# One decode step: row sums of wq, gate, up, w_down and part of wo moved to VectorE, TensorE's projections put into one loop

## The chip, the cores and the metric

The kernel runs on one core of a Trainium2 chip. The core has TensorE (PE), VectorE (DVE), ScalarE (ACT), GpSimd (POOL), a sync engine (SP) that here only issues transfers, and 16 DMA engines that move data between HBM and the on-chip memory (SBUF, 128 partitions). The metric is device time of one execution in microseconds; lower is better. Before the change it is 1362.64 us, the median of 3 runs (1362.63 to 1363.09).

## The reference

One token of one sequence goes through attention over a cached K and V and, beside it, a gated feed-forward layer; all values are float32.

```python
x = A_x                                    # [1, 1, 576]
xn = _layernorm(x, axis=-1)
q = (xn @ wq).reshape(B, Sq, H, Dh)        # wq [576, 4096], H = 32, Dh = 128
scores = einsum("bhqd,bhkd->bhqk", q, k_cache) * (Dh ** -0.5)   # k_cache [1, 32, 16384, 128]
p = softmax(scores, axis=-1)
o = einsum("bhqk,bhkd->bhqd", p, v_cache)
a = o.reshape(B, Sq, H * Dh) @ wo          # wo [4096, 576]
h = gelu(xn @ w_gate) * (xn @ w_up)        # [576, 4608] each
b = h @ w_down                             # [4608, 576]
return x + a + b
```

The two caches are 268 MB each and are read once; all weights together are some 50 MB.

## The kernel before

**Slots.** Three buffers of 64 KB in each partition hold everything large: `sa`, `sb` (K, and weights before and after the heads) and `sv` (V, and weights before the first head). Weight matrices with 576 input rows are cut into 512 rows, four neighbouring ones to a partition (`wmain`, line 188), and the last 64 rows, the *tail*. The tail is folded so that each of its rows fills two partitions (`wtail`, line 189): 128 partitions by half a row.

**Loads.** All large loads go out on SP's queue in program order: wq main into `sa` (line 136), wq tail into `sb` (240), the fourth row and the tail of gate and of up into `sv` (243 to 247), the first three rows of gate into `sb` and of up into `sa` (`ffn`, 328), K of head 0 in two parts into `sb` (386), K of head 1 into `sa` (388), V of head 0 into `sv` (390). Then a loop over heads (391) waits for a free K slot (`s_kf`), loads K, waits for a free V slot (`s_vf`), loads V. After the heads come w_down (28 of its 36 rows into `sb`, line 472; the rest into `sa`, 481, whose last half row per partition is gathered by three small loads to 20 and 8 partitions, 486 to 488) and wo in pieces of 16, 8, 4, 2, 1, 1 rows (497). An engine that waits holds back everything behind it on its queue; SP's waits are those of `o.dma` (line 112) and `take` (360).

**Start.** x comes in on ACT's queue; layernorm runs on one partition; TensorE turns x into columns (288 to 292), and `project` (301) multiplies wq, gate and up by them with 32-column matmuls: 40 calls for wq, 60 each for gate and up, written out one after another. VectorE picks the valid part of each product out of PSUM (334) and reduces it (337).

**Heads.** For each of 32 heads VectorE multiplies K by q (425) and sums over the head dimension (427), takes the maximum (416, 418), ScalarE makes the exponentials (457), TensorE multiplies them by V (411) and folds the result into a column (`out_steps`, 352) in the next turn. TensorE's loop (400) starts at a block boundary of its program (`head_slot`).

**End.** VectorE sums 28 rows of w_down, each scaled by a column of `hT`, into `total` (473 to 476). TensorE multiplies the other rows of w_down (541 to 544) and all 32 rows of wo (545 to 555) by columns of `hT` and `oT`; most accumulate in two halves of 288 columns, the last 12 in four quarters of 144, into which VectorE first adds the halves (550, 551). VectorE and ScalarE copy the quarters out (557 to 562), ScalarE sends the result (563). `release` (149) is a two-turn loop at the end of the programs of VectorE and ScalarE with a branch hint to a place at their start.

**Bookkeeping.** `Order.op` (91) issues an instruction, finds by `needs` (63) what it must wait for and puts the waits on it; `dve`, `act`, `pe_op`, `load` (218 to 236) are short forms.

Of the kernel before, what the change touches and what calls it, by code (L numbers as in the profile page):

```python
# [9 lines left out]
AF = mybir.ActivationFunctionType  # L10
# [14 lines left out]
QG, QB = HD // 4, 512  # L25
QS = HD // 2
# [5 lines left out]
WO_PIECES = (16, 8, 4, 2, 1, 1)  # L32
WO_A = 16
WO_Q = 12
QUART = D // 4
FEW, EACH, RUN = 5, 4, 6
MANY, GROUP = FEW * EACH, EACH * RUN + 1
LEFT = P - FEW * EACH * RUN
AT = 32
SLOT_AT = 28672  # L40
# [3 lines left out]
class Order:  # L44
# [4 lines left out]
    def __init__(self, tc):  # L49
        self.tc, self.nc = tc, tc.nc  # L50
        self.sem = {e: tc.alloc_semaphore(f"s_{e}") for e in ("scalar", "vector", "tensor")}
# [76 lines left out]
def kernel(ctx: ExitStack, tc: tile.TileContext, x, k_cache, v_cache, wq, wo, wg, wu, wd, out):  # L128
# [7 lines left out]
    i = nc.sync.dma_start(slots[0], wq[:DM].rearrange("(p j) f -> p (j f)", j=DJ)).then_inc(ends, 64)  # L136
# [26 lines left out]
def decode(tc, x, k_cache, v_cache, wq, wo, wg, wu, wd, out, slots, s_ends):  # L163
    nc = tc.nc
    o = Order(tc)
    places = [e.mark_branch_hint_location() for e in (nc.vector, nc.scalar)]
# [22 lines left out]
    wtail = {n: w[DM:].rearrange("d (s f) -> (d s) f", s=2) for n, w in (("q", wq), ("g", wg), ("u", wu))}  # L189
# [5 lines left out]
    eps_t, par, same, quarter = sbuf("eps_t", P, 1), sbuf("par", P, 2), sbuf("same", P, 32), sbuf("quarter", P, 4)  # L195
# [11 lines left out]
    row1 = sbuf("row1", 1, D)  # L207
    sel_p, sel_r, sel_l = sbuf("sel_p", P, MANY), sbuf("sel_r", P, RUN), sbuf("sel_l", P, LEFT)
    few_w, few_h = sbuf("few_w", P, RUN), sbuf("few_h", P, RUN + 1)
# [28 lines left out]
    ROW3 = 3 * DF  # L238
    nc.tensor.wait_ge(s_ends, 64).then_inc(s_ends, -64)
    qt = load(sb[:, ROW3 : ROW3 + QS], wtail["q"])  # L240
    row3, tails, at = {}, {}, 0
    for n in "gu":
        s = sem()
        spent.append((s, 48))
        row3[n] = load(sv[:, at : at + DF], wmain[n][:, ROW3:], s, 32)
        tails[n] = load(sv[:, at + DF : at + DF + DF // 2], wtail[n], s, 32)
        at += DF + DF // 2

    xrow = sv[:1, ROW3 + FG : ROW3 + FG + D]
    o.op("vector", lambda e: e.memset(x2, 0.0), x2)  # L250
    s_x = sem()
    o.dma(xrow, xf, s_x, value=49, eng="scalar")
    for i in range(2):
        o.dma(x2[32 * i : 32 * i + 1, :], xf[:, i * HALF : (i + 1) * HALF], s_x, value=49, eng="scalar")
    o.op("vector", lambda e: e.memset(ident, 0.0), ident)
    o.wait("gpsimd", [ident], [ident])
    nc.gpsimd.affine_select(out=ident, in_=ident, compare_op=ALU.not_equal, fill=1.0, base=0,
                            pattern=[[-1, P]], channel_multiplier=1).then_inc(s_x, 1)
    o.note("gpsimd", s_x, 49, [], [ident])
    o.op("vector", lambda e: e.memset(ones, 1.0), ones)  # L260
    o.op("vector", lambda e: e.memset(eps_t, EPS), eps_t)
    s_ap, s_vp, s_pa, s_v, s_vf, s_kf, s_qf, s_qd = (tc.alloc_semaphore(f"h{n}") for n in range(8))
    s_k = [tc.alloc_semaphore(f"k{n}") for n in range(2)]
    for bank, s in ((PO, s_pa), (pc, None), (pq, None)):
        o.op("vector", lambda e, bank=bank: e.memset(bank, 0.0), bank, signal=s)
    dve("tensor_reduce", par, ident.rearrange("p (d s) -> p s d", s=2), axis=AX.X, op=ALU.add)
    dve("tensor_reduce", same, ident.rearrange("p (q r) -> p r q", q=4), axis=AX.X, op=ALU.add)
    dve("tensor_reduce", quarter, ident.rearrange("p (q r) -> p q r", q=4), axis=AX.X, op=ALU.add)

    grouped = ident[:, : FEW * GROUP].rearrange("p (q t) -> p q t", q=FEW)  # L270
    inner = grouped[:, :, : GROUP - 1].rearrange("p q (s r) -> p q s r", s=EACH)
    dve("tensor_reduce", sel_p.rearrange("p (q s) -> p q s", q=FEW), inner, axis=AX.X, op=ALU.add)
    dve("tensor_reduce", sel_r, inner.rearrange("p q s r -> p r q s"), axis=AX.XY, op=ALU.add)
    dve("tensor_copy", sel_l[:, :FEW], grouped[:, :, GROUP - 1])
    dve("tensor_copy", sel_l[:, FEW:], ident[:, FEW * GROUP :])

    stn = nc.vector.BN_STATS_DIM
# [21 lines left out]
    dve("tensor_copy", xtb.rearrange("p (s r) -> p s r", s=2), xt.unsqueeze(2).to_broadcast([P, 2, 32]))

    def project(dst, steps, group, sizes):
        for k, (j, rhs) in enumerate(steps):
            for b, size in enumerate(sizes):
                for q in range(4):
                    lo = q * group + sum(sizes[:b])
                    if j < DJ:
                        lhs = xnb[:, 32 * j : 32 * j + 32]
                    else:
                        lhs = xtb[:, 32 * (q // 2) : 32 * (q // 2) + 32]
                        lo -= q // 2 * 2 * group  # L310
                    pe_op(dst[32 * q : 32 * q + 32, 512 * b : 512 * b + size], lhs, rhs[:, lo : lo + size],
                          k == 0, k == len(steps) - 1)

    project(qb, [(DJ, qt)] + [(j, sa[:, j * HD : (j + 1) * HD]) for j in range(DJ)], QG, (QB, QB))
# [5 lines left out]
    act(qcur, q_part(0))  # L320
    pe_op(pq[:, :DH], ones[:1, :], qcur, True, True)
    act(qs, pq[:, :DH], signal=s_qd)
    act(qcur, q_part(1), signal=s_ap)

    def ffn(which):
        n, t = "gu"[which], (sb, sa)[which]
        steps = [(3, row3[n]), (DJ, tails[n])]
        load(t[:, :ROW3], wmain[n][:, :ROW3])
        project(pg, steps + [(j, t[:, j * DF : (j + 1) * DF]) for j in range(DJ - 1)], FG, FB)
        gm = sv[:, ROW3 : ROW3 + FG].rearrange("p (m t) -> p m t", t=WD_T)  # L330
        at = 0
        for b, size in enumerate(FB):
            m = size // WD_T
            dve("tensor_mul", gm[:, at : at + m, :], pg[:, 512 * b : 512 * b + size].rearrange("p (m t) -> p m t", t=WD_T),
                same[:, at : at + m].unsqueeze(2).to_broadcast([P, m, WD_T]))
            at += m
        dve("tensor_reduce", gu[:, which * WD_T : (which + 1) * WD_T], gm.rearrange("p m t -> p t m"), axis=AX.X, op=ALU.add)

    ffn(0)
    ffn(1)  # L340

    def ffn_act():
        g, u = gu[:, :WD_T], gu[:, WD_T:]
        t1, th, t2 = (tt[:, i * WD_T : (i + 1) * WD_T] for i in range(3))
        dve("tensor_mul", t1, g, g)
        dve("tensor_scalar", t1, t1, 0.044715, 1.0, op0=ALU.mult, op1=ALU.add)
        dve("tensor_mul", t1, t1, g)
        act(th, t1, AF.Tanh, scale=0.7978845608028654)
        dve("scalar_tensor_tensor", t2, th, 1.0, g, op0=ALU.add, op1=ALU.mult)
        dve("scalar_tensor_tensor", hT, t2, 0.5, u, op0=ALU.mult, op1=ALU.mult)  # L350

    def out_steps(h):
        return [(pc[:, :1], z[:, j * DH : (j + 1) * DH], same[:, j : j + 1], j == 0, j == 3) for j in range(4)]
# [6 lines left out]
    def take(e, s, n=1, base=0):  # L360
        e.wait_ge(s, base + n).then_inc(s, -n)  # L361

    def head(h):
        return bass.ds(h, 1)

    ffn_act()
    last_h = hT[:, WD_T - 1 :]
    many, left = slice(AT, AT + MANY), slice(AT, AT + LEFT)
    dve("tensor_scalar", few_w, sel_r, last_h, None, op0=ALU.mult)
    pe_op(pc[many, 8 : 8 + RUN], sel_p, few_w, True, True)  # L370
    pe_op(pc[left, 8 + RUN : 9 + RUN], sel_l, last_h, True, True)
# [103 lines left out]
    for j in range(1, WD_A):  # L475
        dve("scalar_tensor_tensor", total, first[j], hT[:, j : j + 1], total, op0=ALU.mult, op1=ALU.add)
# [119 lines left out]
```

## Time and profile before

| | before |
|---|---|
| time, median of 3 | 1362.64 us |
| span of the profiled execution | 1361.1 us |
| ScalarE busy | 68.7 us (5%) |
| GpSimd busy | 0.5 us, 5 instructions |
| TensorE weight loads | 162.1 us (12%) |
| mean granted TensorE clock | 0.630 of full speed |
| read from HBM | 587.60 MB |

The span runs from the first to the last instruction of one profiled execution; what lies around it is the 1.5 us by which the median is larger. A group in the profile is a line of the kernel, an engine, an operation, and what is written from what (out<-in) with partitions x elements; after a bar come busy time and the mean in nanoseconds. In a timeline a row begins with its start and its length in us. A DMA row gives the size of one transfer in KB of 1024 bytes and the time from issue to landing.

### The profile page before, as it was taken

The numbers are of one execution on the slowest core, as the hardware profiler recorded it, in microseconds if no ns is written. First come the engines' busy times: TensorE is split into PE (matmuls) and PEld (weight loads), VectorE is DVE, ScalarE is ACT, GpSimd is POOL, SyncE is SP. The second block draws the span as 40 slices with busy tenths as digits, with TensorE's granted clock in tenths as the row PEclk, the third lists the DMA queues.
The fourth block names the chain that finished last, engine by engine and source line by source line (L and its number), as shares of the span: only waits on it lengthen the run. The fifth ranks groups of instructions, "written<-read, shape, count | busy, mean of one in ns | idle before, by whom it ended". The sixth has DMA issues, their size and how long they took to land. (4 is left out here: it accounts for less than half of the span.)

```text
span 1361.1 us, 7832 instructions
## 1 busy us (share of the span) xinstructions
PE 449.2 (33%) x3032; PEld 162.1 (12%) x3032; DVE 1163.6 (85%) x210; ACT 68.7 (5%) x238; POOL 0.5 (0%) x5
## 2 busy tenths in 40 slices
PE   2531233323322333323223333233223333332237
PEld 1110111101111111101101111011111111011112
DVE  1069999999888888898888888998888889988884
ACT  0000000000000000000000000000000000000000
POOL 0000000000000000000000000000000000000000
PEclk9765666666556666665566666665566666655668
DMA  9999999999999999999999999999999999999998
GB/s 402 447 424 435 435 443 435 433 431 431 433 433 431 433 435 435 443 435 433 431 431 433 433 431 433 435 435 443 435 433 431 431 433 433 431 433 435 435 446 354
DMA packets 11962, 587.69 MB, mean 432 GB/s; under 512 B 1329, under 2 KB 1715, under 8 KB 1973
## 3 DMA queue, kind: packets, MB, share of 16 engines
q1 hardware_dynamic: 11949, 587.60, 99.7%
q8 instruction: 5, 0.08, 0.0%
q10 hardware_dynamic: 8, 0.01, 0.0%
HBM read 587.60 MB, written 0.00 MB: 432 GB/s over the span
## 5 line engine op out<-in xcount | busy, mean ns | idle before, releaser
L357 PE MATMUL po<-slot_v,pe 128*4 128x512 f32 x2048 | 294.4, 739 | 577.2 <-PEq L361 577.2
L425 DVE TENSOR_TENSOR slot_a<-slot_a,qs 128x16384 f32<-128x16384 f32 x16 | 275.6, 17225 | 34.8 <-DVEq L361 34.8
L425 DVE TENSOR_TENSOR slot_b<-slot_b,qs 128x16384 f32<-128x16384 f32 x15 | 258.4, 17225 | 31.9 <-DVEq L361 31.9
L427 DVE TENSOR_REDUCE scores<-slot_a 128x128 f32<-128x16384 f32 x16 | 275.5, 17220 | 2.3
L427 DVE TENSOR_REDUCE scores<-slot_b 128x128 f32<-128x16384 f32 x15 | 258.3, 17220 | 2.2
L357 PEld LDWEIGHTS po<-slot_v,pe 128*4 128x4 f32 x2048 | 56.7, 99 | 787.8 <-issue 787.8
L404 PE MATMUL pg<-ident,pm 128*1 128x128 f32 x32 | 11.9, 371 | 238.1 <-PEq L361 238.1
L450 ACT ACTIVATE z<-po 128x512 f32<-128x512 f32 x32 | 19.1, 597 | 829.1 <-ACTq L361 829.1
L357 PE MATMUL pc<-same,z 128*128 128x1 f32 x256 | 59.8, 355 | 0.0
L357 PEld LDWEIGHTS pc<-same,z 128*128 128x128 f32 x256 | 57.1, 328 | 0.5
L222 DVE TENSOR_TENSOR slot_v<-pg,same 128x396 f32<-128x396 f32 (+1 forms) x6 | 3.3, 558 | 52.2 <-PE pg L219 52.0
L404 PEld LDWEIGHTS pg<-ident,pm 128*1 128x1 f32 x32 | 2.5, 79 | 243.4 <-issue 243.4
L418 DVE TENSOR_REDUCE nm<-pg 1x1 f32<-1x128 f32 x32 | 8.9, 279 | 21.4 <-DVEq L361 21.4
L357 PE MATMUL pg<-nm,ones 1*128 1x1 f32 x64 | 17.7, 343 | 18.5 <-PEq L361 18.5
L222 DVE SCALAR_TENSOR_TENSOR slot_b<-slot_b,hT 128x576 f32<-128x576 f32 x27 | 22.1, 819 | 0.9
L357 PE MATMUL pqs<-qcur,ones 1*128 1x128 f32 x64 | 14.8, 312 | 21.9 <-PEq L361 20.7
L357 PEld LDWEIGHTS pg<-nm,ones 1*128 1x128 f32 x64 | 15.9, 306 | 27.8 <-issue 27.8
L455 ACT ACTIVATE nb<-pg 128x1 f32<-128x1 f32 x32 | 5.5, 171 | 241.1 <-ACTq L361 241.1
L222 DVE TENSOR_REDUCE scores<-slot_b 128x64 f32<-128x8192 f32 x2 | 17.4, 8686 | 0.1
L222 DVE TENSOR_TENSOR slot_b<-slot_b,qs 128x8192 f32<-128x8192 f32 x2 | 17.4, 8686 | 0.0
L416 DVE TENSOR_REDUCE pm<-scores 128x1 f32<-128x128 f32 x32 | 9.1, 286 | 8.2 <-DVEq L361 8.0
L357 PEld LDWEIGHTS pqs<-qcur,ones 1*128 1x128 f32 x64 | 9.6, 186 | 49.9 <-issue 49.9
(109 smaller groups left out, 158.9 us busy)
## 6 DMA issues: line engine op xcount, KB each, us to landing
slot_b<-in_A_k_cache_dram SPq DMA_DIRECT2D x2, 4096.0 KB, 23.8
slot_b<-in_B_w_down_dram SPq DMA_DIRECT2D x1, 8064.0 KB, 42.0
slot_b<-in_B_w_gate_dram SPq DMA_DIRECT2D x1, 6912.0 KB, 55.3
slot_a<-in_B_w_up_dram SPq DMA_DIRECT2D x1, 6912.0 KB, 37.4
slot_a<-in_A_wo_dram SPq DMA_DIRECT2D x1, 4608.0 KB, 36.5
slot_v<-in_B_w_gate_dram SPq DMA_DIRECT2D x1, 2304.0 KB, 28.8
slot_v<-in_B_w_up_dram SPq DMA_DIRECT2D x1, 2304.0 KB, 35.9
slot_b<-in_A_wo_dram SPq DMA_DIRECT2D x1, 2304.0 KB, 33.4
```

What stands on the lines that cost most here:

```text
L222: o.op("vector", lambda e: getattr(e, name)(out, *ins, **kw), out, *[a for a in ins if isinstance(a, bass.AP)], *[a for a in kw.values() i ...
L357: i = nc.tensor.matmul(dst, lhs, rhs, start=start, stop=stop)
L404: nc.tensor.transpose(pt[:1, :P], pm, ident).then_inc(s_pt, 1)
L416: nc.vector.reduce_max(pm, sc, axis=AX.X).then_inc(s_vp, 1)
L418: nc.vector.tensor_reduce(nm[:1], pt[:1, :P], axis=AX.X, op=ALU.max, negate=True).then_inc(s_vp, 1)
L425: nc.vector.tensor_mul(blk, blk, qs.unsqueeze(1).to_broadcast([P, R, DH])).then_inc(s_d, 1)
L427: nc.vector.tensor_reduce(sc, blk, axis=AX.X, op=ALU.add).then_inc(s_d, 1)
L450: nc.scalar.activation(z, PO, AF.Copy).then_inc(s_ap, 1)
L455: nc.scalar.activation(nb, pb[:, :1], AF.Copy, scale=SCALE).then_inc(s_a, 1)
```

## The change

- The 64 tail rows of wq, gate and up are no longer folded: each fills one partition, so these three loads (1024, 1152 and 1152 KB, as before) go to partitions 0 to 63. The wq tail is the first load; x goes on SP's queue behind it; gate's and up's fourth row and tail share one place in `sv`, so up's wait for gate's to be used.
- VectorE multiplies each weight row by its column of x and adds the rows up (`first`, `more`): five instructions for each of wq, gate and up over 4096 or 4608 elements. The sums lie in `C` (`sv`).
- TensorE adds `C` over the partitions with a matrix of ones, in one loop of three turns (wq, gate, up), 12 matmul calls a turn; a fourth semaphore counts hand-overs (`s_c`, `s_g`).
- GpSimd adds up what VectorE picked from PSUM (a tree of five additions for gate and for up), and computes gelu's arithmetic.
- In TensorE's head loop the folding of a head's result comes after its V product, in the same turn; the loop no longer starts at a block boundary.
- w_down's last 8 rows and wo's first 12 rows go to VectorE's `total` (`gather`); wo comes in pieces of 12, 8, 6, 4, 1, 1 rows; TensorE's quarters take the last 6. The three small loads are gone.
- The softmax sums are scaled once per partition by a matmul with `lx`; `oT` is scaled by VectorE.
- `release` is called for TensorE too. TensorE's program has 486 instructions.

```diff
-WO_PIECES = (16, 8, 4, 2, 1, 1)
-WO_A = 16
-WO_Q = 12
+WO_PIECES = (12, 8, 6, 4, 1, 1)
+WO_D, WO_A, WO_Q = 12, 20, 6
...
-    i = nc.sync.dma_start(slots[0], wq[:DM].rearrange("(p j) f -> p (j f)", j=DJ)).then_inc(ends, 64)
+    i = nc.sync.dma_start(slots[2][:TAIL, T_AT : T_AT + HD], wq[DM:]).then_inc(ends, 64)
...
-    wtail = {n: w[DM:].rearrange("d (s f) -> (d s) f", s=2) for n, w in (("q", wq), ("g", wg), ("u", wu))}
...
+    r3, tail, C = sv[:, :DF], sv[:TAIL, T_AT : T_AT + DF], sv[:, C_AT : C_AT + DF]
+    qt, q0 = sv[:TAIL, T_AT : T_AT + HD], sv[:, T_AT : T_AT + HD]
...
+    o.dma(xrow, xf, s_x)
+    load(sa, wmain["q"])
+    load(sb[:, : 3 * DF], wmain["g"][:, : 3 * DF])
...
+    def more(out, row, j, acc):
+        dve("scalar_tensor_tensor", out, row, xp[: row.shape[0], j : j + 1], acc, op0=ALU.mult, op1=ALU.add)
+    def first(row):
+        dve("tensor_scalar", row, row, xp[:, 0:1], None, op0=ALU.mult)
...
+    dve("tensor_scalar", qt, qt, x5, None, op0=ALU.mult)
+    more(rows[0], rows[0], 0, q0)
+    more(rows[0], rows[1], 1, rows[0])
+    more(rows[0], rows[2], 2, rows[0])
+    more(CQ[:, :, :QW], rows[3].rearrange("p (g c) -> p g c", g=4), 3, rows[0].rearrange("p (g c) -> p g c", g=4))
+    tell("vector", s_c, 2)
+    load_rest("g")
+    first(rows[0])
+    more(rows[0], rows[1], 1, rows[0])
+    more(rows[0], r3, 3, rows[0])
+    more(rows[0][:TAIL], tail, DJ, rows[0][:TAIL])
+    nc.vector.wait_ge(s_g, 1)
+    more(C, rows[2], 2, rows[0])
+    tell("vector", s_c)
+    load(sa[:, : 3 * DF], wmain["u"][:, : 3 * DF])
+    load_rest("u")
+    first(rows[0])
+    nc.vector.wait_ge(s_g, 2)
...
+            gps("tensor_add", dst, gm[:, :n], gm[:, n : 2 * n])
...
+    spread(0)
+    tell("vector", s_c)
+    more(C, rows[1], 1, rows[0])
+    more(C, rows[2], 2, C)
+    more(C, r3, 3, C)
+    more(C[:TAIL], tail, DJ, C[:TAIL])
+    tell("vector", s_c)
+    with nc.Fori(0, 3, engines=OrderedEngineSet([KIND["tensor"]])):
+        take(nc.tensor, s_c, 2)
+        for b, size in enumerate(FB):
+            for q in range(4):
+                lo = q * FG + sum(FB[:b])
+                i = nc.tensor.matmul(pg[32 * q : 32 * q + 32, 512 * b : 512 * b + size], ones[:, :32], C[:, lo : lo + size], start=True, stop=True)
+        i.then_inc(s_g, 1)
+        take(nc.tensor, s_t)
+        nc.tensor.matmul(pq[:, :DH], ones[:1, :], qfirst, start=True, stop=True).then_inc(s_b, 1)
...
+    nc.sync.wait_ge(s_g, 3)
     o.wait("sync", [], [sv])
     load_v(0)
...
+    nc.vector.wait_ge(s_g, 3)
+    spread(1)
...
+    with nc.Fori(0, H, engines=OrderedEngineSet([KIND["tensor"]])):
...
-        chain(out_steps(0), s_pa)
-        take(nc.tensor, s_ap)
         take(nc.tensor, s_v, 16)
         chain([(PO[32 * (k % 4) : 32 * (k % 4) + 4, :], pe[:, 4 * k : 4 * k + 4], sv[:, 512 * k : 512 * k + 512], k < 4, k >= 28)
                for k in range(32)], s_pa)
         nc.tensor.drain().then_inc(s_vf, 1)
+        take(nc.tensor, s_ap)
+        chain(out_steps(), s_pa)
...
-    o.dma(few[:, : RUN * HALF], by_q[:, : GROUP - 1, :], s_x, value=97)
-    o.dma(few[:FEW, RUN * HALF :], by_q[:, GROUP - 1, :], s_x, value=97)
-    o.dma(few[FEW:LEFT, RUN * HALF :], src[FEW * GROUP :], s_x, value=97)
...
+    rows = load_rows(sb, 0, wdv, 0, WD_A)
+    total = gather(rows, hT, None)
     take(nc.sync, s_vf)
     load_v(H - 1)
     take(nc.sync, s_kf)
+    gather(load_rows(sa, 0, wdv, WD_A, WD_T - WD_A), hT[:, WD_A:], total)
...
+    pe_op(pl, lx, ones[:, :1], True, True)
+    dve("reciprocal", rl, pl)
+    nc.vector.wait_ge(s_o, H)
+    dve("tensor_mul", onx.rearrange("p (h r) -> p h r", r=4), oall.unsqueeze(2).to_broadcast([P, H, 4]),
         quarter.unsqueeze(1).to_broadcast([P, H, 4]))
     pe_op(po, onx, same, True, True)
+    dve("tensor_scalar", oT, po, rl, None, op0=ALU.mult)
+    gather(wo_rows[:WO_D], oT, total)
+    halves = [(oT[:, j : j + 1], wo_rows[j]) for j in range(WO_D, WO_T - WO_Q)] + [(ones[:, :1], total)]
+    for n, (lhs, w) in enumerate(halves):
+        add_half(lhs, w, last=n >= len(halves) - 2)
...
+    release(nc, KIND["tensor"], nc.tensor, places[2])
```

More of the change, by code (lines that the diff above doesn't have):

```diff
@@ L260, in decode @@
[L260 to L266, printed above, removed]
@@ new lines, in decode, with load_rest @@
+    nc.vector.wait_ge(s_ends, 64).then_inc(s_ends, -64)
+    dve("tensor_scalar", qt, qt, x5, None, op0=ALU.mult)
+    rows = [sa[:, j * HD : (j + 1) * HD] for j in range(DJ)]
+    more(rows[0], rows[0], 0, q0)
[3 more added lines that the diff above has]
+    tell("vector", s_c, 2)
+    def load_rest(n):
+        s = sem()
+        spent.append((s, 48))
+        load(r3, wmain[n][:, 3 * DF :], s, 32)
+        load(tail, {"g": wg, "u": wu}[n][DM:], s, 32)
@@ L318, in q_part, with out_steps @@
         return qb[r : r + 1, lo : lo + DH]
[L320 to L352, printed above, removed]
+    nc.scalar.wait_ge(s_g, 1)
+    cuts = sorted({0, 512, QW, *(sum(FB[:b]) for b in range(1, 3))})
+    for lo, hi in zip(cuts, cuts[1:]):
+        b = max(b for b in range(3) if sum(FB[:b]) <= lo)
+        at = 512 * b + lo - sum(FB[:b])
+        act(qb[:, lo:hi], pg[:, at : at + hi - lo])
+    act(qfirst, q_part(0))
+    tell("scalar", s_t, 3)
+    nc.scalar.wait_ge(s_b, 1)
+    act(qs, pq[:, :DH])
+    tell("scalar", s_c)
+    tell("scalar", s_qd)
+    act(qcur, q_part(1))
+    tell("scalar", s_ap)
+    def out_steps():
         return [(pc[:, :1], z[:, j * DH : (j + 1) * DH], same[:, j : j + 1], j == 0, j == 3) for j in range(4)]
@@ L358, in chain @@
         i.then_inc(s, 1)
-    def take(e, s, n=1, base=0):
-        e.wait_ge(s, base + n).then_inc(s, -n)
     def head(h):
         return bass.ds(h, 1)
[L366 to L371, printed above, removed]
-    act(few_h[left, RUN:], pc[left, 8 + RUN : 9 + RUN])
-    act(few_h[many, :RUN], pc[many, 8 : 8 + RUN])
-    o.wait("tensor", [ident, ones, same], [pg, pc, PO, pq])
-    o.wait("vector", [qs], [S, pm, nm])
-    o.wait("scalar", [qb], [z, qs, nb, pe, lsum, oall, qcur])
     def load_k(h, dst, s):
@@ L396, in decode @@
             load_v(i * 2 + (1 + s))
-    (s_a, a_base), (s_pt, pt_base) = o.step("scalar"), o.step("tensor")
-    with nc.Fori(0, H, engines=OrderedEngineSet([KIND["tensor"]]), head_slot={KIND["tensor"]: 0}):
+    take(nc.vector, s_qd)
+    for src, sc in parts:
+        blk = src.rearrange("p (n d) -> p n d", d=DH)
+        dve("tensor_mul", blk, blk, qs.unsqueeze(1).to_broadcast([P, SUB, DH]))
+        dve("tensor_reduce", sc, blk, axis=AX.X, op=ALU.add)
+    tell("vector", s_kf)
+    tell("vector", s_qf)
+    nc.vector.wait_ge(s_g, 3)
+    spread(1)
+    g, u = gu[:, :WD_T], gu[:, WD_T:]
+    t1, th = (tt[:, i * WD_T : (i + 1) * WD_T] for i in range(2))
+    gps("tensor_mul", t1, g, g)
+    gps("tensor_scalar", t1, t1, 0.044715, 1.0, op0=ALU.mult, op1=ALU.add)
+    gps("tensor_mul", t1, t1, g)
+    o.wait("tensor", [ident, ones, same], [pg, pc, PO, pq])
+    o.wait("vector", [], [pm, nm])
+    o.wait("scalar", [], [z, nb, pe, ls, lx, oall])
+    s_pt, pt_base = o.step("tensor")
+    with nc.Fori(0, H, engines=OrderedEngineSet([KIND["tensor"]])):
         take(nc.tensor, s_ap)
```

211 lines of the change are left out of this document (86 added, 125 removed).

## The prediction

> **What bounds the kernel now.** The page comes first: its span, the busiest engines and the transfers.
>
> ```profile
> span 1361.1 us, 7832 instructions
> ...
> PE 449.2 (33%) x3032; PEld 162.1 (12%) x3032; DVE 1163.6 (85%) x210; ACT 68.7 (5%) x238; POOL 0.5 (0%) x5
> ...
> q1 hardware_dynamic: 11949, 587.60, 99.7%
> q8 instruction: 5, 0.08, 0.0%
> ```
>
> The queue that carries all large loads has kept the 16 DMA engines busy for 99.7% of the span. VectorE, the busiest engine, is busy for 85%. The stretches say whether that holds everywhere:
>
> ```profile
> 25.00:140.00 115.00, 46.49 (x384) 16.59 (x387) 60.20 (x25) 4.36 (x14) 0.00 (x0) 0.67 1.01 436
> 140.00:500.00 360.00, 117.45 (x731) 42.30 (x724) 334.58 (x40) 18.95 (x68) 0.00 (x0) 0.61 1.00 434
> 500.00:1250.00 750.00, 234.74 (x1467) 84.67 (x1467) 680.18 (x77) 38.26 (x137) 0.00 (x0) 0.61 1.00 435
> ```
>
> The columns are stretch, its length, PE, PEld, DVE, ACT and POOL with counts, granted clock, DMA share and GB/s. The rate is 434 to 436 GB/s in the projections (25 to 140 us), where DVE is busy for only 60.20 of 115 us, and through the heads. 435/16 is 27.2 GB/s for one engine. It is a ceiling: neither the work on chip nor the matrix being read moves it. The chain of work that ended last, and ScalarE's timeline at the end, close the picture:
>
> ```profile
> 1325.11 32.33 DMA slot_b<-in_A_wo_dram
> ```
> ```profile
> 1358.31 0.28 ACT L227 ACTIVATE row<-pqs 1x144 f32<-1x144 f32 x1 [13.56 <-PE pqs L219]
> 1358.69 0.28 ACT L227 ACTIVATE row<-pc 1x144 f32<-1x144 f32 x1
> 1359.01 0.24 ACTq L563 DMA_DIRECT2D out_dram<-row  x1
> ```
>
> The last piece of wo lands at 1357.44. Two final half rows, a copy and the 2.2 KB result follow, some 3.7 us. So the time is bytes over 435 GB/s plus a start of about 2 us and this end. The bytes do not change (all weights and caches are read once). What can change the time is therefore (1) the rate at which a transfer runs, (2) what else uses the DMA engines, (3) a compute step so late that SP's queue runs dry, (4) the end. Work taken off PE is worth nothing by itself.
>
> **The change part by part.** All sums are made against the profiled execution's 1361.1 us; the median of the runs lies 1.5 us higher, and I carry that difference over unchanged.
>
> *The tails (1).* The three tail loads, their KB and the us from issue to landing, in the transfer list of the first 100 us:
>
> ```profile
> slot_v<-in_B_w_gate_dram SPq DMA_DIRECT2D x1, 1152.0 KB, 31.1
> slot_v<-in_B_w_up_dram SPq DMA_DIRECT2D x1, 1152.0 KB, 39.5
> slot_b<-in_A_wq_dram SPq DMA_DIRECT2D x1, 1024.0 KB, 23.7
> ```
>
> Together 3328 KB, 3.41 MB, at 435 GB/s 7.8 us. Now they reach 64 partitions instead of 128. No row shows what that does: every large load of before reaches all 128. Bounds: if the ceiling belongs to the 16 engines and they stay evenly loaded, nothing (0 us). If it belongs to the receiving memory, or if engines are dealt out by partition, half of it is left, and each tail takes twice its time: +2.4, +2.7, +2.7, in all +7.8 us. A gain has no reason. The queue is full before and after each tail, so none of it can hide behind other transfers. The nearest rows are the stretches above: one ceiling for all shapes and loads, met only with all partitions in use. Of the three readings (memory side, engines by partition, engines alone) two give the upper end, and I take it: **+7.8 us**.
>
> [...]
>
> *Program and small loads (2).* The page's q8 row has 5 packets of 0.08 MB, 16 KB each: program, and of the engines only PE has a program of thousands of instructions. Spread evenly over 16 engines at 432 GB/s they cost 0.2 us; all on one engine of 27.2 GB/s, 3.0 us, for a load has landed only when its slowest engine is through. A program of 486 instructions should need none or one on the way. The three small w_down loads (144 KB to 20 and 8 partitions) vanish into a 128-partition load; being on few engines they cost up to about 1 us there. I take **−1.0 us** for both together, near the case in which the packets fell on different engines (0.6 us each on the engine that ends last), with ends of 0 and −3.
>
> [...]
>
> *VectorE's sums at the start (3).* Prices by operation and tile, then the first heads in the timeline:
>
> ```profile
> L222 DVE SCALAR_TENSOR_TENSOR slot_b<-slot_b,hT 128x576 f32<-128x576 f32 x27 | 22.1, 819 | 0.9
> ...
> L222 DVE TENSOR_TENSOR slot_b<-slot_b,qs 128x8192 f32<-128x8192 f32 x2 | 17.4, 8686 | 0.0
> ...
> L222 DVE TENSOR_TENSOR slot_v<-pg,same 128x396 f32<-128x396 f32 x4 | 2.3, 570 | 52.1 <-PE pg L219 52.0
> ...
> L222 DVE TENSOR_SCALAR slot_b<-slot_b,hT 128x576 f32<-128x576 f32 x1 | 0.5, 520 | 2.0 <-DMA slot_b<-in_B_w_down_dram 2.0
> ...
> L257 POOL TENSOR_SCALAR_AFFINE_SELECT ident<-ident 128x128 f32<-128x128 f32 x1 | 0.3, 293 | 2.0 <-DVE eps_t L261 2.0
> ```
> ```profile
> 1.53 0.34 SPq L116 DMA_DIRECT2D slot_b<-in_A_wq_dram  x1
> ...
> 123.31 0.35 SPq L379 DMA_DIRECT2D slot_b<-in_A_k_cache_dram  x1
> ...
> 133.76 9.16 PE L357 MATMUL po<-slot_v,pe 128*4 128x512 f32 x64 [6.80 <-PEq L361]
> ...
> 159.41 0.33 SPq L379 DMA_DIRECT2D slot_a<-in_A_k_cache_dram  x1
> ```
>
> An added element costs 1.04 ns (8686 ns for 8192, 819 for 576 less some 220 fixed), so a multiply-add over 4608 takes 5.0 us, over 4096 4.5; the scaling of a row between 2.8 (the slope of the shorter rows) and 4.7, I take 2.8. wq: four behind its landing, 18.0 us (the tail's scaling is done before). Gate: 2.8 + 4 x 5.0 = 22.9. Up: 22.9 and three products from PSUM, 1.7. In all 65.5 us. Before, these stages held PE instead, and DVE stood idle. wq's two loads landed at 25.2 (1.53 + 23.7); with a slow first tail 27.6. The sums then end near 91, or near 96 where they wait for up's delayed load; K of head 0 (4 x 8.69 = 34.8) is done at 126, or 131. Then SP may issue K of head 2. The load ahead of it, V of head 0, lands where PE starts on it, 133.7, or 141.5 with the tails' delay. [...] Against 123.31 before, DVE starts 3 to 8 us later into the heads and catches up there: between K2 and the next K load it needs 36.1 us a head (123.31 to 159.41), and 16.8 MB at 435 GB/s take 38.6. Cost **0**, hidden by the queue; without the margin each us late is a us. Of the moved loads, tail and fourth row of up wait for gate's sums (about 63) and K0 for the last gate row (68); SP's queue then still holds up's main load. PE's loop turns are short (12 calls, where gate had 60), and K1 waits only for up's rows in `sa`. GpSimd's trees are 2 x 1116 elements; at 2.3 ns (293 ns for 128) 2.6 us each, inside the margin even where they block VectorE.
>
> *Heads.* Folding behind the V product starts no load later: `s_vf` is still signalled behind the product, and PE then waits for VectorE's next maximum. **0.**
>
> *The end (4).* VectorE's own timeline of before:
>
> ```profile
> 1311.76 0.52 DVE L222 TENSOR_SCALAR slot_b<-slot_b,hT 128x576 f32<-128x576 f32 x1 [1.99 <-DMA slot_b<-in_B_w_down_dram]
> 1312.31 23.02 DVE L222 SCALAR_TENSOR_TENSOR slot_b<-slot_b,hT 128x576 f32<-128x576 f32 x27
> 1336.15 0.36 DVE L222 TENSOR_SCALAR slot_a<-slot_a,few_h 20x288 f32<-20x288 f32 x1 [0.82 <-DMA slot_a<-in_B_w_down_dram]
> 1336.55 3.22 DVE L222 SCALAR_TENSOR_TENSOR slot_a<-slot_a,few_h 20x288 f32<-20x288 f32 x6
> 1343.14 0.36 DVE L222 RECIPROCAL small<-pg 128x32 f32<-128x32 f32 x1 [3.36 <-PE pg L219]
> 1343.53 0.19 DVE L222 TENSOR_TENSOR tt<-oall,small 128x32 f32<-128x32 f32 x1
> 1343.75 0.29 DVE L222 TENSOR_TENSOR z<-tt,quarter 128x128 f32<-128x128 f32 x1
> 1353.82 0.94 DVE L222 TENSOR_TENSOR x<-x,qb 64x288 f32<-64x288 f32 x2 [9.77 <-PE qb L219]
> ```
>
> A row costs 23.02/27 = 0.85 us. On this clock: w_down's last 8 rows from 1336.2 to 1343.0; reciprocal, product, matmul and scaling of `oT` to about 1344.8; wo's first 12 rows, 3.5 MB behind w_down, are there by 1344.5 and end at 1355.0; PE adds `total`, VectorE the halves, 1356.4. The last two wo rows, 0.59 MB, land over the last 1.4 us, from 1356.8 to 1358.2. So VectorE is done just before PE needs it: **0**, with a margin of about 1 us; beyond it, each us late is a us.
>
> Sum: 1361.1 + 7.8 − 1.0 = 1367.9 for a profiled execution, **1369.4 us** for the median.
>
> **The rivals.** *Half the partitions at full rate* (not slower): if the engines alone carry the ceiling, place and price are the three tails at 0 us instead of 7.8, and 1361.6 is left. For it: the rows show 27.2 GB/s an engine whatever is read. Against it: none shows this with fewer partitions. It decides from a rate for the tails above 295 GB/s (extra under 3.7 us), where the total stays within 2.7 us of before. [...] *The program does not stay:* the head loop, no longer aligned, crosses a block, and each of 32 turns fetches one or two blocks of 16 KB: 0.5 to 1 MB, 1.2 to 2.4 us, so 1364 at full rate, 1371.5 with slow tails. For it: five fetches before, in straight code; against it, the loop of before ran 32 turns without any.
>
> **How the numbers follow.** A measurement of this kernel can tell about 0.2%, 2.7 us, from no change. Forecast 0.66; tails at full rate 0.24; VectorE late 0.05 and program fetched 0.05, half of each with slow tails. Slower by over 0.2% (above 1365.4): 0.66 + 0.04 = 0.70. Within: 0.22 + 0.06 = 0.28. Faster (below 1359.9) needs the fetches at their 3.0 us and full rate: 0.02. The forecast's own range is 1366.5 to 1371.0 (tails +5.5 to +8, fetches 0 to −1.5); that holds some 0.6, so the range reaches down to the full-rate case at 1361.3.
>
> **What would show it.** Right: the rate between 0 and 75 us falls in three places, stretches without waits on SP; K0 and V0 land 5 to 8 us later; from 140 us on all is shifted, at 434 GB/s; q8 has 0 to 2 packets. Full rate: 436 GB/s from 25 to 140 us, V0 at about 133. VectorE late: the DMA share dips near 135, or PE waits for `total` at the end while loads have landed. Program fetched: dozens of q8 packets. Wrong would be above all a full-rate tail.

## The result, and the profile after

| | before | after |
|---|---|---|
| median | 1362.74 us (6 runs, 1362.63 to 1363.09) | 1376.1 us (6 runs, 1371.73 to 1529.68) |
| profiled execution | span 1361.1 us | 1371.73 us, span 1369.8 |

The change makes the kernel slower by less than one per cent: after over before is 1.0092, with a 95% interval from 1.0071 to 1.0112. Three of the six executions lie apart, at 1379.8, 1380.6 and 1529.7 us (the ratio holds the first two of them); what follows explains the others, and the last experiment is about these three. The others, here and in four later series, take 1371.5 to 1373.0 us: 9 to 10 us more than before, where 6.8 were forecast.

The page of the changed kernel, span, engines and queues:

```profile
span 1369.8 us, 7222 instructions
...
PE 393.1 (29%) x2667; PEld 124.0 (9%) x2667; DVE 1236.6 (90%) x223; ACT 77.5 (6%) x274; POOL 47.5 (3%) x23
...
q1 hardware_dynamic: 11618, 587.60, 99.7%
q8 instruction: 1, 0.02, 0.0%
```

The bytes are the same and the queue is as full as before. PE lost 56 us of work and DVE gained 73, and neither sets the time. One program fetch is left of five. Stretches of the changed kernel (columns as before: stretch, length, PE, PEld, DVE, ACT, POOL, clock, DMA share, GB/s); the first two lie inside the tails of gate and of up:

```profile
49.00:53.00 4.00, 0.96 (x10) 0.29 (x2) 4.00 (x1) 1.86 (x7) 0.00 (x0) 0.94 1.08 221
77.00:80.00 3.00, 0.00 (x0) 0.00 (x0) 3.00 (x1) 0.00 (x0) 3.00 (x1) 0.50 0.97 197
...
25.00:140.00 115.00, 13.69 (x83) 5.30 (x83) 106.04 (x27) 4.09 (x12) 26.80 (x9) 0.65 1.01 413
140.00:500.00 360.00, 115.57 (x766) 35.57 (x767) 341.95 (x38) 25.29 (x80) 15.43 (x5) 0.61 1.00 434
500.00:1250.00 750.00, 219.73 (x1468) 69.08 (x1468) 677.60 (x80) 40.73 (x158) 0.74 (x3) 0.61 1.00 434
```

Inside the tails the engines are as busy as ever (share 0.97 to 1.08) and move 197 to 221 GB/s, about half of 435. No engine is idle; each packet of the tails takes up to 2.15 times its time at 27.2 GB/s. From 140 us on the rate is that of before, 434.

The trace's packet records give the cost. A packet's own duration, less its bytes over 27.2 GB/s, summed and divided by 16, is the excess in us of the whole queue:

```
stretch (us)        before    after
0 to 28               0.94     2.82
48 to 56              0.03     3.00
71 to 83              0.12     3.08
sum of the three      1.09     8.90
```

The difference is 7.8 us. The rest of the loss shows at the end. VectorE's timeline of the changed kernel, then what PE (its weight loads, PEld) waits for behind its half rows, then ScalarE's timeline:

```profile
1352.51 10.21 DVE L216 SCALAR_TENSOR_TENSOR slot_b<-slot_a,oT,slot_b 128x576 f32<-128x576 f32 x12 [0.28 <-DMA slot_a<-in_A_wo_dram]
1364.32 1.01 DVE L216 TENSOR_TENSOR x<-x,qb 64x288 f32<-64x288 f32 x2 [1.60 <-PE qb L213]
```
```profile
1364.79 0.09 PEld L213 LDWEIGHTS pg<-slot_b,oT 128*1 128x1 f32 x2 [0.66 <-DMA slot_b<-in_A_wo_dram]
```
```profile
1367.64 0.52 ACTq L572 DMA_DIRECT2D out_dram<-slot_v  x1
```

By the landing records the last half row of wo is there at 1366.2 (one engine; the other 15 have theirs by 1364.9), before at 1358.16. The output leaves 1.4 us behind it, before 0.85 us (1359.01). So the 8.7 us of the spans are 8.0 at the last landing and 0.6 behind it.

What lies behind it is PE's work. Its half rows end at 1364.7, and the piece with rows 26 to 29 of wo is there at 1364.75, 1.44 us ahead of the last landing. From then PE works without a gap until 1366.9: four quarter rows, x, the last two rows, 2.1 us in all. In the kernel before, the piece ahead of the last two rows has two rows instead of four, and PE is through with it at 1357.43, as the next row lands (1357.44).

### The profile page after: what moved, and what is told of

The parts are those of the page before. It is cut to its first block, busy times and chain, and to the rows that moved or that the text cites. A ratio compares the mean times of both kernels' runs of the same rounds, so it can differ in the third digit from the quotient of the medians.

```text
span 1369.8 us, 7222 instructions
## 1 busy us (share of the span) xinstructions
PE 393.1 (29%) x2667; PEld 124.0 (9%) x2667; DVE 1236.6 (90%) x223; ACT 77.5 (6%) x274; POOL 47.5 (3%) x23
## 5 line engine op out<-in xcount | busy, mean ns | idle before, releaser
L386 PE MATMUL pc<-same,z 128*128 128x1 f32 x256 | 32.7, 249 | 29.1 <-PEq L239 29.1
L235 POOL TENSOR_TENSOR gm<-gm 128x576 f32<-128x576 f32 (+3 forms) x8 | 36.4, 4552 | 106.7 <-DVE gm L216 105.9
L386 PEld LDWEIGHTS pc<-same,z 128*128 128x128 f32 x256 | 31.0, 191 | 57.9 <-issue 57.9
L357 PE MATMUL pg<-slot_v,ones 128*32 128x396 f32 (+1 forms) x72 | 10.8, 764 | 75.8 <-PEq L239 75.8
```

The lines of the kernel that those rows point to most:

```text
L235: o.op("gpsimd", lambda e: getattr(e, name)(out, *ins, **kw), out, *[a for a in ins if isinstance(a, bass.AP)], *[a for a in kw.values() i ...
L357: i = nc.tensor.matmul(pg[32 * q : 32 * q + 32, 512 * b : 512 * b + size], ones[:, :32], C[:, lo : lo + size], start=True, stop=True)
L386: i = nc.tensor.matmul(dst, lhs, rhs, start=start, stop=stop)
```

## The experiments

Times of the kernel before beside these runs: 1362.75 to 1362.84 us (medians of the five series).

### The tails folded again: fold

The changed kernel, with the tails of wq, gate and up loaded to 128 partitions as before, and two half rows added by VectorE.

```diff
-        load(tail, {"g": wg, "u": wu}[n][DM:], s, 32)
+        load(tail, {"g": wg, "u": wu}[n][DM:].rearrange("d (s f) -> (d s) f", s=2), s, 32)
...
-    more(C[:TAIL], tail, DJ, C[:TAIL])
+    fold(C, tail, DF // 2)
```

> The three tails go to 128 partitions as before (half a row each), VectorE adds two half rows where it added one; everything else as changed. Half-rate tails: the shortest execution falls by 7 to 8 us, to 1364 to 1365, and the rate between 25 and 100 us is 435 GB/s again. Rival, full-rate tails with the loss elsewhere (VectorE late at the start, the end): within 1.5 us of 1371.7. The scatter, if it has nothing to do with the tails, stays.

Measured: 1365.81 us (11 runs, 1364.91 to 1366.9), ratio 1.0023 [1.0014, 1.0032]. The same two stretches of this kernel:

```profile
49.00:53.00 4.00, 0.45 (x2) 0.29 (x2) 3.96 (x2) 1.18 (x5) 0.00 (x0) 0.91 1.03 445
77.00:80.00 3.00, 0.00 (x0) 0.00 (x0) 2.96 (x2) 0.00 (x0) 2.87 (x1) 0.50 1.21 524
```

The half rate is gone. (A short stretch counts whole packets where they end, so 524 is not a rate by itself; with each packet counted for the part that falls into the stretch, both have 433 to 434 GB/s, and the changed kernel 206 to 215.) That gives back 6.3 us, not the 7 to 8 expected. What is left, 3 us over before, is in part something that the slow tails had hidden. SP's timeline, K of heads 2 and 3, first of the changed, then of the folded kernel:

```profile
132.64 0.35 SPq L393 DMA_DIRECT2D slot_b<-in_A_k_cache_dram  x1
...
171.91 0.33 SPq L393 DMA_DIRECT2D slot_a<-in_A_k_cache_dram  x1
```
```profile
130.45 0.34 SPq L401 DMA_DIRECT2D slot_b<-in_A_k_cache_dram  x1
145.87 0.34 SPq L404 DMA_DIRECT2D slot_v<-in_A_v_cache_dram  x1
169.99 0.33 SPq L401 DMA_DIRECT2D slot_a<-in_A_k_cache_dram  x1
```

In the changed kernel V of head 0 is there at 140.1 us by the landing records, 7.5 us after K of head 2 was asked for. In the folded kernel it is there at 133.0, 2.6 us after. That is too late: the first of the 16 engines is through with V at 131.5, and K's first packet starts at 131.57, 1.1 us behind its issue. The engines run thin there, and again behind 170 us: between 100 and 500 us the packet records show 0.5 us without packets (mean of the 16 engines) and 1.3 us more excess than before.

### VectorE earlier: foldearly

VectorE's timeline of the folded kernel around up's sums shows where it loses time, then GpSimd's, its trees:

```profile
67.27 2.62 DVE L216 TENSOR_SCALAR slot_a<-slot_a,small 128x4608 f32<-128x4608 f32 x1 [0.16 <-DVE slot_v L216]
71.44 1.49 DVE L216 TENSOR_TENSOR gm<-pg,same 128x396 f32<-128x396 f32 x3 [1.55 <-PE pg L365]
73.07 6.16 DVE L216 SCALAR_TENSOR_TENSOR slot_v<-slot_a,small 128x4608 f32<-128x4608 f32 x1
79.26 5.43 DVE L216 SCALAR_TENSOR_TENSOR slot_v<-slot_a,small,slot_v 128x4608 f32<-128x4608 f32 x1
84.72 5.12 DVE L216 SCALAR_TENSOR_TENSOR slot_v<-slot_v,small 128x4608 f32<-128x4608 f32 x1
```
```profile
73.02 17.03 POOL L235 TENSOR_TENSOR gm<-gm 128x576 f32<-128x576 f32 x4 [70.41 <-DVE gm L216]
90.19 2.43 POOL L235 TENSOR_TENSOR gu<-gm 128x36 f32<-128x36 f32 x1
```

It waits 1.55 us for gate's product from PE, and while GpSimd's tree runs beside it (73 to 93 us) three of its multiply-adds take 6.16, 5.43 and 5.12 us instead of 5.02. The edit puts up's second row into the wait; a second one gives PE four of VectorE's rows of wo.

```diff
     first(rows[0])
+    more(rows[0], rows[1], 1, rows[0])
     nc.vector.wait_ge(s_g, 2)
...
-    more(C, rows[1], 1, rows[0])
-    more(C, rows[2], 2, C)
+    more(C, rows[2], 2, rows[0])
...
-WO_D, WO_A, WO_Q = 12, 20, 6
+WO_D, WO_A, WO_Q = 8, 20, 6
```

> The changed kernel with the tails folded to 128 partitions (1365.8 us in the earlier run), and two moves: VectorE adds up's second row before it waits for gate's product (a wait of 1.55 us there), and it sums 8 rows of wo instead of 12, PE taking the other 4. If VectorE is late at the start, K of head 2 is issued near 128.9 us instead of 130.45 and that of head 3 near 168.4 instead of 170.0, both ahead of the last packets queued before them; the transfers no longer run thin at 133 and 171 us (together about 1.8 us in the folded kernel), and with up to 0.6 us at the end the time comes to 1363.5 to 1364.5. If the 2 to 3 us that the folded kernel still lacks lie elsewhere (bytes per packet, the program fetch near 145 us), it stays at 1365 to 1366.

Measured: 1364.08 us (11 runs, 1363.76 to 1365.06), ratio 1.0010 [1.0001, 1.0019]. SP's timeline:

```profile
128.03 0.34 SPq L401 DMA_DIRECT2D slot_b<-in_A_k_cache_dram  x1
143.22 0.34 SPq L404 DMA_DIRECT2D slot_v<-in_A_v_cache_dram  x1
167.57 0.33 SPq L401 DMA_DIRECT2D slot_a<-in_A_k_cache_dram  x1
```

Both K loads are asked for 2.4 us earlier, the excess between 100 and 500 us falls from 2.88 to 1.75 us (before: 1.61), and the last packet ends at 1358.08 instead of 1359.59 us (before: 1357.87). So VectorE was late at the start: at full-rate tails it costs 1.5 us. The output's issue stays 1.4 us behind the last landing, so the four rows of wo that PE took over did not matter there. With full-rate tails and a VectorE in time, the last packet still ends 0.2 us later than before the change.

### The end: foldend, foldq

Beside the edits of foldearly, the piece of wo's rows 26 to 29 is cut in two (foldend), then 12 instead of 6 rows of wo are also added by quarters on PE (foldq).

```diff
-WO_PIECES = (12, 8, 6, 4, 1, 1)
+WO_PIECES = (12, 8, 6, 2, 2, 1, 1)
...
-WO_D, WO_A, WO_Q = 8, 20, 6
+WO_D, WO_A, WO_Q = 8, 20, 12
```

> The folded kernel with the earlier second row and 8 rows of wo on VectorE (1364.1 us), and the piece of wo's rows 26 to 29 cut in two. PE began these rows only 1.4 us before the last ones were there, and the output left 1.55 us after the last packet, against 0.85 us before the change. If the rest of the gap to the kernel before (1.2 us) lies in this end: 1363.3 to 1363.7, the output's issue within 1.1 us of the last landing. If not: 1364.1.

> The folded kernel with the earlier second row, 8 rows of wo on VectorE, the small last pieces, and now 12 of wo's rows added by quarters instead of 6 (0.13 us a row on PE against 0.42 to 0.50 by halves). In the two kernels before it PE's halves ended at 1356.7 to 1357.2, VectorE's sum for x 0.7 to 1 us behind them, and PE's last rows came late. If PE's half rows make the end late: the sum for x ends near 1355.5, the output leaves within 1.0 us of the last landing instead of 1.5, and the time is 1363.2 to 1363.6. If the end is bound by the last landings alone: 1364.1.

Measured: foldend 1364.07 us (4 runs, 1363.25 to 1364.58), ratio 1.0009 [0.9995, 1.0023]; foldq 1364.15 us (11 runs, 1363.05 to 1365.8), 1.0009 [1.0000, 1.0018]. VectorE's sum for x and the output's issue, of foldend and of foldq:

```profile
1356.78 1.01 DVE L216 TENSOR_TENSOR x<-x,qb 64x288 f32<-64x288 f32 x2 [5.30 <-PE qb L213]
```
```profile
1359.82 0.52 ACTq L580 DMA_DIRECT2D out_dram<-slot_v  x1
```
```profile
1353.88 1.01 DVE L216 TENSOR_TENSOR x<-x,qb 64x288 f32<-64x288 f32 x2 [2.57 <-PE qb L213]
```
```profile
1359.18 0.52 ACTq L580 DMA_DIRECT2D out_dram<-slot_v  x1
```

The smaller pieces alone did nothing: foldend's PE adds half rows until 1357.16, and the sum for x comes at 1356.78. (In foldearly PE had ended them at 1356.29 and waited for the piece of four rows, there at 1356.94; the granted clock was 1.00 in 24 of these multiplications, 0.65 in the same ones of foldend.) With quarters the sum for x is 2.9 us earlier, PE waits at each landing, and the output leaves 0.9 us behind the last one (1358.24) instead of 1.4 (1358.42). So the late end is PE's work behind the last pieces, 0.5 us, and in the profiled executions it went only when pieces and half rows were both cut; quarters with the piece of four rows were not run. The median does not move: foldq's other spans reach from 1361.1 to 1363.3, and 1.75 to 2.7 us lie outside them (before 1.75 to 1.9). Where that comes from stays open. No version here beats the kernel before.

### Loads to 64 partitions, in the kernel before: v64, v128

Only V of head 0 is cut: its last quarter (2.10 MB) goes as two loads to 64 partitions each, in the control as two loads by columns to all 128. GpSimd waits for the three parts and signals.

```diff
-    load_v(0)
+    load_v0()
...
+        nc.sync.dma_start(sv[:, :c], src[:, :c]).then_inc(s, 16)
+        for p in (slice(0, 64), slice(64, P)):
+            nc.sync.dma_start(sv[p, c:], src[p, c:]).then_inc(s, 16)
```

> The kernel before, in which only the load of V of head 0 is cut: three quarters of its columns as before to 128 partitions, the last quarter as two loads to partitions 0 to 63 and 64 to 127 (1.05 MB each; same bytes, same places). GpSimd, idle, waits for the three and passes the signal on. At half rate for the two: +4.8 us, 1367.6; at full rate 1363. Theory of the step: no program fetch comes between this load's end (about 138 us) and 1347 us, so nothing brings the engines out of step: in some executions the slow mode lasts to the end, and they take 100 us and more longer; the others 1367 to 1368. Theory of an outside disturbance: all executions within 1 us of each other, at 1367 to 1368.

> Control for the kernel above: the last quarter of V of head 0 is cut into two loads by columns instead, both to all 128 partitions (same bytes, same count of loads, same signals). Both theories: the time of the kernel before, 1362.8 within 0.5 us, and no execution that lies apart.

Measured: v64 1370.36 us (5 runs, 1369.26 to 1370.75), ratio 1.0054 [1.0040, 1.0068]; v128 1362.91 us (11 runs, 1362.72 to 1363.19), 1.0001 [0.9992, 1.0010]. Same bytes, same signals: the count of partitions alone costs 7.5 us, where 4.8 were expected. By the packet records 7.3 us of it are excess between 100 and 500 us (9.0 against 1.75). A stretch inside the two loads of v64:

```profile
127.00:137.00 10.00, 0.72 (x4) 0.63 (x3) 10.00 (x1) 0.39 (x2) 0.00 (x0) 0.50 1.12 224
```

Half rate again, but 7.5 us are more than the 4.8 of doubled packets. The 16 KB packets of these loads took 2.1 times their time in the middle and up to 3.1 times, and 16 of the 64 KB packets of the next load, to all partitions, took up to 1.8 times theirs while some engines were still at the 64-partition loads. So these loads also slowed what ran beside them.

### Executions that lie apart: again, head, nohint, unstep, fold64

Three causes were tried for the executions of 1378 us and more. The first: TensorE's program is fetched anew. `head` starts TensorE's head loop at a block boundary again, `nohint` leaves out the hint and its loop at TensorE's end.

```diff
-    with nc.Fori(0, H, engines=OrderedEngineSet([KIND["tensor"]])):
+    with nc.Fori(0, H, engines=OrderedEngineSet([KIND["tensor"]]), head_slot={KIND["tensor"]: 0}):
```
```diff
-    places = [e.mark_branch_hint_location() for e in (nc.vector, nc.scalar, nc.tensor)]
+    places = [e.mark_branch_hint_location() for e in (nc.vector, nc.scalar)]
...
-    release(nc, KIND["tensor"], nc.tensor, places[2])
```

> The changed kernel itself, unaltered. If its scatter (1371.7 to 1529.7 us) belongs to the kernel, the executions here fall again near 1372, near 1380 and perhaps far above, while the kernel before stays within 1 us. If the scatter was a disturbance of that one series, all executions lie within 3 us of 1372.

> TensorE's head loop starts at a block boundary again, as before the change; nothing else is altered. If the scatter comes from TensorE's program (its head loop lies across two blocks and is sometimes fetched again), all executions lie within 3 us of 1372 here, with one or two program packets for the end of the program. If it comes from GpSimd and VectorE waiting for each other, or from elsewhere, 1380 and more appear again.

> TensorE's release loop and the branch hint at its start are taken out; the head loop stays unaligned. If the hint keeps TensorE's program in place, its loss brings many program packets (dozens) and times of 1380 and above in most executions. If the hint itself causes the scatter, all executions lie within 3 us of one another. If neither, the scatter stays as in the changed kernel.

Measured: again 1371.8 to 1372.3, and 1528.4, 1533.4 (6 runs; ratio 1.0067 [1.0053, 1.0082]). Head 1371.8 to 1372.3, and 1378.4, 1531.7 (6 runs; 1.0079 [1.0064, 1.0094]). Nohint 1371.8 to 1372.3, and 1380.2, 1532.9, 1608.5, 1665.3 (8 runs; 1.0083 [1.0064, 1.0102]). The profile of nohint is of its longest execution, and it has two fetches; the two others, of executions that do not lie apart, have one. So no stream of fetches made it long, and head, with its loop at a block boundary, has executions apart as well. Stretches of that longest execution:

```profile
49.00:53.00 4.00, 0.86 (x10) 0.29 (x2) 4.00 (x1) 1.87 (x7) 0.00 (x0) 0.92 1.09 221
57.00:70.00 13.00, 0.00 (x0) 0.00 (x0) 12.93 (x3) 0.00 (x0) 0.00 (x0) 0.50 0.91 340
85.00:95.00 10.00, 0.00 (x0) 0.00 (x0) 9.93 (x3) 0.00 (x0) 9.83 (x2) 0.50 0.93 328
...
500.00:1250.00 750.00, 172.04 (x1176) 53.35 (x1179) 552.01 (x65) 32.47 (x126) 0.74 (x3) 0.59 1.00 354
```

Up to gate's tail it is like the others. Behind that tail each packet takes 1.17 times its time (373 GB/s by the packet records, 340 as the stretch counts whole packets), behind up's tail 1.23 times, and so to the end, with all engines busy.

The second theory was that loads to 64 partitions bring the 16 engines into step (at 120 us their packets end within 0.3 us of each other, in the kernel before within 1.6), and that engines in step can stay slow. `unstep` puts a small load to 8 partitions behind the two tails to part them. The third was VectorE's and TensorE's new work: `fold64` is the folded kernel with unread loads to 64 partitions.

```diff
         load(tail, {"g": wg, "u": wu}[n][DM:], s, 32)
+        load({"g": sb, "u": sa}[n][:8, 3 * DF : R * DH], {"g": wg, "u": wu}[n][DM : DM + 8, : R * DH - 3 * DF])
```
```diff
+        for lo, w in ((T_AT + DF // 2, DF // 2), (X_AT + D + 2 * TAIL, R * DH - X_AT - D - 2 * TAIL)):
+            load(sv[:TAIL, lo : lo + w], {"g": wg, "u": wu}[n][DM:, :w])
```

> The changed kernel, with its three loads to 64 partitions as they are. Behind the tails of gate and up, one more small load each is added: 8 partitions of 10 KB into unused columns (82 KB each, 0.2 us of the queue if spread, some 0.4 to 0.8 us on the engines that carry it). Theory of the step: the loads to 64 partitions bring the 16 DMA engines into step (their packets start within 0.3 to 0.4 us of each other, against 0.8 to 2.1 us in the kernel before), and some executions stay in a slow mode from there; engines put out of step again leave it. By it the shortest time stays at 1372 to 1373 us and no execution lies above 1375. Theory of an outside disturbance, or of a cause that the small load does not touch: 1372 to 1373 for the shortest, and a third to a half of the executions at 1378 and more, as in every kernel with these loads so far.

> The changed kernel again, as a control beside the next two on the same chip. So far 11 of the 26 executions of kernels with its 64-partition tails lay 6 us and more above the shortest. Expected: 1371.7 to 1372.4 for the undisturbed ones, and two or three of six to eight above 1378.

> The changed kernel with a small load to 8 partitions behind the tails of gate and of up, a second time, for more executions: four of four lay at 1375.0 to 1375.5 before, which at 11 slow ones in 26 would be chance one time in nine. If the small load keeps the engines out of the slow mode: all at 1375 to 1375.6 again. If that was chance: a third to a half at 1381 and more.

> The folded kernel (no slow execution in 11, 1365.8 us) with loads that nobody reads: behind each of the tails of gate and up two more loads to partitions 0 to 63, into free columns (1.06 MB together each time). VectorE's and TensorE's work is that of the folded kernel. At half rate they cost 2 x 4.9 = 9.8 us, of which the 1.8 us of late issues at 133 and 171 us come back: 1373 to 1376. If the loads to 64 partitions make the slow executions: again a third to a half of them lie 6 us and more above the shortest. If it was VectorE's or TensorE's new work on 64 partitions, or chance: none.

> The changed kernel as control of the next two on this chip. If this chip is like the first: a third to a half of the executions 6 us and more above the shortest, 1372. If like the last: all at 1371.5 to 1372.4, and the next two then say nothing on the slow executions.

> The changed kernel with a small load to 8 partitions behind the tails of gate and up. If the control scatters: all at 1374 to 1375.6 by the theory of the step; a third to a half above 1380 if the step has no part in it.

> The folded kernel with unread loads to 64 partitions behind the tails of gate and up: 1374.5 to 1375.0 undisturbed. If the control scatters and the loads to 64 partitions are the cause: it scatters too, to 1381 and more. If the control scatters and VectorE's or TensorE's work on 64 partitions is the cause: it does not.

> The changed kernel as control. If this chip is like the first: a third to a half of the executions 6 us and more above 1372. If like the other three: all at 1371.5 to 1373.1.

> The folded kernel with unread loads to 64 partitions: 1374.1 to 1375.0 undisturbed. If the control scatters and these loads are the cause, it scatters too (1381 and more); if the control scatters and VectorE's or TensorE's work is the cause, it does not; if the control does not scatter, nothing follows.

Measured, in four further series:

| kernel | executions (us) | ratio |
|---|---|---|
| unstep | 1375.0 to 1375.5 (4) | 1.0092 [1.0076, 1.0107] |
| again2 | 1371.5 to 1372.2 (4) | 1.0066 [1.0051, 1.0080] |
| unstep2 | 1374.2 to 1374.6 (4) | 1.0084 [1.0070, 1.0099] |
| fold64 | 1374.5 to 1375.0 (4) | 1.0088 [1.0073, 1.0102] |
| again3 | 1371.7 to 1373.0 (5) | 1.0070 [1.0056, 1.0084] |
| unstep3 | 1374.4 to 1375.5 (3), 1379.3 | 1.0099 [1.0084, 1.0115] |
| fold64b | 1374.1 to 1375.0 (5) | 1.0085 [1.0070, 1.0099] |
| again4 | 1371.9 to 1372.3 (5) | 1.0068 [1.0054, 1.0082] |
| fold64c | 1373.9 to 1376.0 (4) | 1.0090 [1.0075, 1.0106] |

The controls again2, again3 and again4 showed no execution apart, the last one on the very chip on which again had shown two of six. So nothing follows from fold64, and the one 1379.3 of unstep3, whose small loads part the engines (1.4 us at 120 us in its profiled execution), speaks against the theory of the step. The count: of kernels with loads to 64 partitions 11 of 26 executions lay apart in the first two series and 1 of 44 in the later ones; of kernels without them none of 34 and none of 89. Only kernels with these loads showed it, and the loads are not enough for it; the cause, and whether it lies in the kernel at all, stays open.

What these runs do settle is the price of loads. Fold64's unread loads are 2.13 MB at 4.9 us of full rate. They cost 8.9 us against the folded kernel, and 1374.7 − 1364.1 = 10.6 us against the one without its late start (foldearly), which slow loads hide: a little over twice the bytes' time, a third kernel for the half rate. Unstep's 0.16 MB cost 2.2 to 3.1 us (its medians less those of again, again2 and again3; unstep and again ran on different chips) where 0.4 to 0.8 were expected for a load: its 10 KB packets took 1.9 to 3.5 times their time, and packets of the next load, to all partitions, up to 2.5 times.

## Why the prediction was right in one step and wrong in the sum

- **Tails, +7.8.** Right in size: 7.8 us by the packet records, 197 to 221 GB/s with all engines busy, and undone by folding them. The mechanism was left open among three readings, and the size taken because two of them gave it. The runs leave one: all 16 engines work, so the ceiling is not with the engines alone, and they are not dealt out by partition either, for then half of them would stand idle (their share in the tails is 0.97 to 1.08). What is left of the three is the receiving side; that is an inference, no run shows it by itself.
- **Program and small loads, −1.0.** Wrong, and the largest miss. The program did shrink to one fetch, as forecast, and that gained nothing. The last packet ends 8.02 us later (1357.87 to 1365.89), so beside the tails there is +0.2 instead of −1.0. What counts is the last engine. At 145 us the packets of all 16 end within 0.3 us of each other; the one fetch left, at 149.17, takes an engine 0.97 us, and from then to the end one engine is 1.3 to 1.5 us behind the other fifteen. In the kernel before the engines are spread over 2.0 us at the end. The mean of the sixteen last landings moved by 7.6 us, the last one by 8.0, which fits that the fetches that are gone helped the mean and not the last; no run brings them back one by one, so this part is argued. The forecast laid the gain on the engine that ends last without a row that says so. What the three small loads had cost by themselves no run shows.
- **VectorE's sums at the start, 0.** Right for this kernel, by another sum than the one given, and the slow tails covered the error: K of head 2 was issued at 132.64 (131 in the forecast), 7.5 us ahead of V of head 0. The margin was wrong, and no run shows it at full rate: K of head 0 was to end at 126 and V of head 0 to be there at 133.7; folded, VectorE ended K of head 0 at 130.1, V was there at 133.0, and 1.5 us were lost. The margin was also taken to the last engine's landing, while the first engine runs dry 1.5 us earlier. From issue to first packet K of head 2 took 1.1 us in the folded kernel; the first load took 1.0 us before the change (0.73 to 1.75) and 1.3 us after it (0.75 to 2.09). Of the sums, up's were wrong, 27.8 us instead of 24.6: a wait for PE that had no price (1.55 us), and GpSimd's tree, which made VectorE's multiply-adds 1.65 us longer. Each tree was priced at 2.6 us; the four adds before the last took 17.0 us, and 20.3 the second time. The second tree of the changed kernel, which runs partly beside VectorE's product of K (137.03 to 154.26):

```profile
L235 POOL TENSOR_TENSOR gm<-gm 128x72 f32<-128x72 f32 x1 | 17.1, 17147 | 0.1
L235 POOL TENSOR_TENSOR gm<-gm 128x576 f32<-128x576 f32 x1 | 1.4, 1395 | 36.8 <-DVE gm L216 36.8
L235 POOL TENSOR_TENSOR gm<-gm 128x288 f32<-128x288 f32 x1 | 0.8, 789 | 0.1
L235 POOL TENSOR_TENSOR gm<-gm 128x144 f32<-128x144 f32 x1 | 0.5, 487 | 0.1
```

  The three larger adds began ahead of that product, 1.40 us for 576 elements, 2.4 ns an element: the price of 2.3 ns was about right. The add of 72 elements began 0.3 us behind the product and took 17.15 us, until 0.2 us after its end. In the first tree the adds of 288, 144, 72 and 36 elements took 5.32, 5.02, 4.87 and 4.83 us, each until shortly after the end of the multiply-add that VectorE had begun before it, and VectorE's first multiply-add, begun 0.06 us behind the add of 576, took 1.1 us longer. Beside VectorE's sum with one operand, from 154.40 us, the last add took 0.26 us. So an instruction of VectorE with two operands in SBUF and an add on GpSimd took turns here, whatever the add's size. "Inside the margin even where they block VectorE" left out that an add waited through a whole instruction of VectorE.
- **Heads, 0.** Right: 434 GB/s from 140 us on.
- **End, 0.** Wrong by +0.6. VectorE's sums end at 1362.7, 3.5 us ahead of the last landing (3.2 in the forecast). The step counted VectorE's time and gave PE's none: behind the half rows and the piece of four rows PE needs 2.1 us, and the last landing is 1.44 us away. Foldq, with smaller pieces and more quarter rows, gets 0.5 us of it back in its profiled execution.
- **Outside the span.** The forecast carried 1.5 us over unchanged; the profiled execution has 1.93. Most of that is no effect of the change: the 1.5 was a median less the span of one execution, and in the five later series 1.74 to 1.94 us lie outside the span of the kernel before as well.

The forecast's sum with these sizes is 1361.1 + 7.8 + 0.2 + 0.6 = 1369.7 for the span, measured 1369.8, and 1371.7 with 1.93; as the 0.2 is what was left over, this is bookkeeping and no test. The range ended at 1371.0, because it took the gains of a shrunken program from −0 to −1.5 and no cost at the end. The median of 1376.1 is beyond any of its cases: none of them had executions that lie apart.

## What to carry to other kernels

In these runs a load to half the partitions cost 2.0 to 2.5 times the time of its bytes, and two loads to 8 partitions 6 to 8 times (2.2 to 3.1 us for 0.16 MB, 0.38 us at 435 GB/s), also by slowing their neighbours in the queue: fold short matrices over all 128 partitions even where the sums then need one instruction more (6.3 us here). Fewer interruptions of the transfers may gain nothing while one engine still has one (one program fetch instead of five gained nothing, and one engine was 1.3 us and more behind to the end); ask which engine lands last. Work moved to an idle engine is not free when it runs beside a busy one (GpSimd's tree made VectorE's multiply-adds 1.65 us longer): see whether the two take turns, and add the waits between the engines (1.55 us for PE) to the margin. A margin that holds only because something else is slow shows when that is mended (1.5 us, folded).

## What was not expected of the hardware

- GpSimd's adds and VectorE's instructions with two operands in SBUF took turns: an add of 72 elements a partition took 17.15 us beside a product of 17.23 us, and a multiply-add 6.15 us instead of 5.02 behind an add of 1.39 us.
- Two small loads to 8 partitions (0.16 MB) cost 2.2 to 3.1 us.
- In one execution all 16 engines stayed busy, behind loads to 64 partitions, at 354 instead of 434 GB/s for the remaining 1.6 ms; it was not brought about at will.
